# Key-weight transposes on TensorE, x tiles ahead on SyncE's queue, and a new order table in a two-attention kernel

## Chip, core and metric

One core of a Trainium2 chip. The metric is the device time of one launch in microseconds (us): the median of the runs of a kernel. The profiled execution is a run of its own, taken with the hardware profiler.

## What is computed

Two attention blocks on the same sequence of S = 2048 rows and D = 640 columns (32 heads of 20), mixed row by row by a gate. Cut to what matters:

```python
g = sigmoid((x * gate_w).sum(-1))            # one gate a row
# A: linear attention with a learned feature map
q, k, v = split(x @ wqkv)
pq, pk = q_h @ w_phi_h, k_h @ w_phi_h        # a 20x20 map for each head
phi = concat(softmax(p), softmax(-p))        # for pq and pk
a = (phi_q @ (phi_k^T v)) / (phi_q @ sum(phi_k)) @ A_wo
# B: 4 segments of 512 rows: causal softmax attention in the segment,
#    and a memory M, z of the segments before, read with elu(q)+1
b = (sigmoid(beta) * mem(q) + (1 - sigmoid(beta)) * softmax_attn(q, k, v)) @ B_wo
out = g * a + (1 - g) * b
```

## The kernel before

**Where things live.** x is held transposed in SBUF (`xT`, five blocks of 128 columns by 2048 rows). Tiles 0 to 3 (128 rows each) arrive as plain loads in `x_nat` and are transposed on TensorE against an identity matrix, five 128x128 blocks a tile into one PSUM bank (L681), then copied to `xT` on ScalarE or VectorE (L691, L693). Tiles 4 to 15 come by DMA transposes from DRAM (L569). Of PSUM's eight banks, four are one score tile (`st4`) and four (`w_76` to `w_79` in the profile) rotate among everything else.

**Block B.** `seg_in` projects a segment's four tiles on WkB, WqB and WvB (`proj`, L745: five matmuls of 320 columns for a half of the width); keys and queries are written to DRAM (`kd`, L764) and read back transposed (`kqT`, L1109). `b_qk` (L1138) makes scores into `st4`, one ScalarE exponential of 128x2048 turns them into `PT` (L1144), GpSimd masks the diagonal blocks (L1150), and `b_pv` (L1166) multiplies by the values.

**Block A.** The map w_phi is folded into the weights: for the keys, `WkA` = Wk x blockdiag(w_phi). A matmul wants the raw weights transposed as its stationary operand, so `wt_load` (L564) fetches them into `WT` by five DMA transposes of 128 columns each; `fold` (L730) makes ten groups of three matmuls against `WphiD`, the block-diagonal map that VectorE builds from `Wc` and a mask (L667), and ScalarE or VectorE evicts each group (L710, L712). The same happens for the queries later, through the same `WT`. `a1` projects the tiles on WvA and WkA, and `a3_num` and `fin` make the outputs.

**What sets the order.** Every operation is registered with an engine, a planned duration, what it reads and writes, and a number in the order of registration. `ORDER` is a table written out in the file: for each engine, the numbers in the order in which that engine shall run them ("73*3" is 73, 74, 75). The planner walks through these lists with its durations, gives each PSUM user the bank that is free first, and emits instructions in the order of the planned times. The engines run their own lists strictly in order and wait on semaphores. DMAs from SyncE (SP) and one from ScalarE use eight completion semaphores in turn, so that the ninth DMA waits for the first to land.

**The start.** ScalarE issues the first half of WkB. SP issues x tiles 0, 1, 2, then gate_w, half of WqB, Wc, beta, x tile 3, then the other halves of the weights. PE runs seven warm-up matmuls of 512 columns on a zeroed tile (L588) before tile 0 is transposed, and three more between the tiles.

Of the kernel before, what the change touches and what calls it, by code (L numbers as in the profile page):

```python
# [9 lines left out]
BF16 = mybir.dt.bfloat16  # L10
# [3 lines left out]
P = 128  # L14
# [13 lines left out]
        "29*7 73*3 77*2 80 88 104 89 82 120 90*2 105 121 92 106 94 122 95 107 123 96 108 124 126 "  # L28
        "97*2 127*2 136 129*2 137 110*2 142 112 138 113 143 114 144 139 192 145 193 140 146 176*2 "
        "194 178 195*2 84 208*2 179 210 224 170 225 180 226 171 227 211 228 212 164*2 172 166*2 "  # L30
        "173 152 174 158 153 168 154 159 155*2 160 182 161 230*2 183 261 232 162 184 262 185 263 "
        "186 233 264*2 234 362 426 363 427 364*3 428 368 400 369 429*2 464 401 465 402 198 370 "
        "403 199 371 200 372 404 201 466 509 214 202 247*2 215 467 216 249*2 254*2 468 256 251 "
        "257 512 258 458 217 240 218 241*2 459*4 243*2 394*2 276*3 292*3 396 284*3 397*2 308*3 "
        "288 280 312*2 289*2 314 296 281 297 282 298 661*3 838 664 839 665 840*2 749 842 750 655 "
        "751 656 300*2 657 304*2 302 306 516 752*2 374 658 375 381*2 659 376*2 383 378 384 406 "
        "385 527 814*2 649 816*2 650 818 413 651 414 407 415 408 416 409 417 520 410 521*2 652 "
        "530 523 671*2 438 673 439 674 445*3 440 448 675 441*2 543 449 693 703*3 694 706 695 707 "
        "696 709*4 775*2 697 777 477*2 778 479*2 779 481 546 470 713 471 534*3 472*2 537 474 850 "
        "857 851 858 852 859 853 860 854 550 861 687 828 688 829*2 737 689 738 690 677 739 691 "  # L40
        "740 678*2 741 680 831 681 832 743*2 561 882 745 883 746 889 884 747 885 890*2 886 892 "
        "876 893 877*2 564 879*2 432 921 433 914 434 915 922 435 923*2 436 916 925 719*4 577 490 "
        "917 554*3 491*2 723 493 557 918 494*2 499 496 500*3 580 902 953 903 954*2 904 908 905 "
        "909 934 956 910 906 957 911*2 584 935 568*4 946*2 1229 948 1230 949 1231 950 936*3 595 "
        "1232 1203 1233 940 791 941 1204*2 942 792 943 1206 944 1210 793 1207 1211*2 794 1213*2 "
        "598 1197 795 844 1198*2 845 725 846 1200 1342*3 847 1201 726 848 1345*2 611 727*3 588*3 "
        "870 591 807*3 975 810 976 871 977*2 614 811 602 872*2 603*2 874 605 731 643*4 618 732*4 "
        "966 759*2 967 761 968*2 1352 970 1353 971 762 972 763 629 1354*2 1261 1235*2 1262 1356 "
        "1242 1237 1263*2 1243 1238 1265 1244*2 781 1239 1246 632 622 782*2 623*2 1287*2 784 "
        "797*3 785 625 1289*2 800 1557*2 1291 1559 801 1560*2 995 1255*4 1267 1259 1268 1274 1269 "  # L50
        "1275 1270*2 1276*2 821 1278 822*2 998 1519*3 824*2 636*3 1522*2 639 1299*2 1446 1301*2 "
        "1430 1303 1447*2 1002 1431 1449*2 1432 1306*2 1433 1488*2 1308 1434 1490 1309 1491 1310 "
        "1492 1531 1017 765*4 1532 1538*2 1533 769 1540 1368*2 1534*2 1541*2 1020 1570*3 1370*3 "
        "1374*2 1006 1376*3 1007*4 1573*2 1563*5 1043 1384*3 1595 1387*2 1596 1223 1597 1602 "
        "1598*2 1224 1603*2 1225 1605 1226 1191 1606 1227 1192 1046 1193 1293 1194 1294 1336 1295 "
        "1025 1337 1026 1296*2 1027 1195 1338 1028 1339*2 1024 1319*7 1050 2409*5 1615 1462*2 "
        "1616*2 1464*2 1618 1634 1619 1466 1065 1328*4 1621 1635 1622 1589 1636*2 1623 1638 1590 "
        "1624 1591 1068 1592 1625 1055*2 1054 1057 1593 1058 1424*4 1091 1627*4 1390 1631 1428 "
        "1583 1391 1584*2 1392 1586 1179 1393 1587 1394 1094 1180*2 1358 1182 1359*2 1073 1361 "
        "1074*3 1362 1551 1072 1552*4 1098 2435*3 334*3 2438 330*3 322 2439 326 323 327 324 338 "  # L60
        "328 339*2 1113 346*3 350 342 351 343 1478 352 344 1479*3 1185*3 1482 1188 358*2 354*2 "
        "360 1116 356 1103*4 1102 1418*2 1412 1420*3 1413 1139 1525*3 1414 1528 2416*2 1529 2418 "
        "1415 1121 1416 2419 1122 2420 1123*2 1647*2 1120 1649 1656 1650 1657*2 1651*2 1659 1653 "
        "1142 1440*4 1472 1444 1473 1406 1474 1407*2 1502 1475*2 1503 1409*2 1495 1146 1504 1496 "
        "1505 1497 1506 1509*2 1498 2442 1499 1511*3 1456*2 1161 1458 2492 1459 2443 2493 1460 "
        "2444 2498 2445 2494 2446 2495*2 1670 1164 1400 2461*2 1401 2463 1666 2499 1402 2464 2500 "
        "2465 2501*2 1151 1403 1152 1672 1153 1668 2103 1154 1695*2 1404 1697*2 1169 1699 1170*2 "
        "1150 2106 1172 1681*3 1168 1684*2 1688*5 2110 2531*5 1709 1716 1710 1726*2 1717*3 1711 "
        "1728 1712 1729 2545 1713 2546*3 2125 1702*3 2549 1705 1759*4 2115*2 1706 2117*2 2114 "
        "2128 1888*3 1737 1891 1738 1892 1747*2 1739 2403 1749*2 2404 1740 2405*3 2151 2422*5 "  # L70
        "1769*4 2132*5 2154 2485*5 1780*2 1790 1782*2 1791*3 2479*5 2158 2467*5 1812 1802*2 1813 "
        "1804 1814*2 1805 2429*3 2505*2 2432*2 2173 2507*3 1895*3 1823*2 1898 1825*2 1899 1833*4 "
        "2511*3 2176 2514*2 2163*3 2162 2524 2166 2525*4 2455*4 2199 2459 1902*2 1866*4 1904*2 "
        "2180 1906 2181*4 2202 1845*4 1909*4 1855*2 1913 1857*2 1916*4 2206 1920 2552*4 2289 2556 "
        "2290 1876 2291 1877*3 2292*5 1923 2297*2 2221 1924*3 2301*3 1954*2 2304*4 1956*2 2308*3 "
        "2327*3 1944 2330*2 1945 1933*2 1946*2 2332 1935*2 2333*4 2224 2518*2 2448 2520 2449 2521 "
        "2450 2522 2451 2473*3 2452 2476*2 2247 2210 1987*3 2211 1990 2212*3 2229*4 2250 2391*4 "
        "2379*3 2228 2382*5 1976*2 2387*2 2254 1966 1978 1967*2 1979 1969 2341*3 2397*2 2344*5 "
        "2399 2349*2 2400 2269 2538*2 2315 2540 2316 2541 1997*2 2009 1999*2 2010 2317 2011 2318 "
        "2012 2542 2319*3 2272 2322*2 2019 2324 2020*3 2259*4 2258 2885 2787*9 2040*2 2796 2042*2 "  # L80
        "2030*4 2367*2 2888 2369*5 2062 2374 2063 2375 2064 2376 2065 2052*3 2277*2 2055 2279 "
        "2892 2594*2 2280 2596*2 2276 2598 2573*5 2775*3 2073*4 2907 2566*3 2083*2 2569*2 2085*2 "
        "2778*4 2897*2 2782 2899 2783 2900 2910 2784 2896 2580*3 2353*2 2583*2 2355*6 2601*2 2933 "
        "2603*2 2361*2 2611 2587 2612*3 2588*3 2915 2591 2916*3 2914 2936 3076*2 2801 3078 2802 "
        "3079 2803 2632 3080 2633*3 2622*2 2804 2624*2 2805*6 2940 3069 2644*4 2654 3070 2655*3 "
        "3071*3 2675*4 2955 2665*4 3083*3 2687*3 3086 2690 3087 2697*4 2958 2827*9 2708 2836 "
        "2709*3 2853*6 2718 2859*2 2719*3 2861*2 2981 2730 2740 2731 2741*3 2732 3090*3 2733 "
        "3093*2 2945*4 2984 2944 2963*4 2962 2865*4 2988 2869*5 2751*4 2813 2874 2814 3104 2815*3 "
        "3105 2818*3 3106*2 2821*2 3003 3097 2761*3 3114 2764 3098 3115 3099 3116*2 3100*2 2993*4 "
        "3006 2992 3278*3 3147 3281*2 3148 3283 3149 3284*3 3150 3287 3125*4 3029 2839*4 3135*2 "  # L90
        "2843 3137*2 2844*4 3157 2848 3158*3 3290*2 3032 3168*4 3292*4 3304*2 3296 3306 3297*3 "
        "3307*3 3178*4 3310 3200 3311 3201*3 3312*2 3190*4 3036 3011*4 3010 3211*4 3051 3221*4 "
        "3330*10 3233*3 3054 3243 3236 3244*3 3041*3 3316*3 3044 3319*5 3040 3324*2 3368*5 3254*4 "
        "3373 3264*4 3374*3 3059*2 3377 3061*2 3058 3342*6 3356*4 3348 3360 3349 3361 3350 3362*2 "
        "3351 3364*2 3381 3462 3435 3408 3383*6 3395 3389 3396 3422 3390 3397 3423 3391 3398*2 "
        "3410 3392 3400 3424*2 3401 3426 3411 3427 3412 3402*2 3428 3404 3429 3413 3430 3414 "
        "3449*2 3415 3431 3451 3437 3452 3416 3453 3438 3417 3454 3439 3455 3464 3418 3465 3456 "
        "3440 3466 3419 3457 3441 3467 3458 3442 3468*3 3443 3471 3444 3476 3472 3445 3477*2 3473 "
# [1290 lines left out]
```

The softmax here doesn't subtract the row's maximum and nothing guards it: scores larger than these inputs give would overflow.

## Time and profile before

| | |
|---|---|
| median of 3 runs | 291.14 us (291.12 to 291.29) |
| profiled execution | 290.81 us, of which the span of the trace is 289.1 |
| granted TensorE clock | 1.00 |
| TensorE (PE) busy | 281.2 us, 3777 matmuls |
| ScalarE (ACT) busy | 246.9 us |
| VectorE (DVE) busy | 229.6 us |
| GpSimd (POOL) busy | 189.0 us |
| SP's DMA queue | 37.39 MB, 58.5% of 16 DMA engines |

PE is the matmul engine and PEld its weight loads, which overlap it. "SPq" lines are DMA issues. A row of the timeline gives start, duration, engine, line, operation, tiles and shapes, and in brackets how long the engine had been idle before it and what ended that. A row of the windows gives a stretch, its length, the busy time of PE, PEld, DVE, ACT and POOL with the number of instructions, the granted clock, the DMA engines' share and GB/s. Matmuls are pipelined and their ends are modelled, so the spacing of their starts says more than their length. A tile's number in the profile is that of a buffer (`w_76` to `w_79` are the four banks, `st_75` is `st4`, `PT_119` a buffer of `PT`).

### The profile page before, as it was taken

The numbers are of one execution on the slowest core, as the hardware profiler recorded it, in microseconds if no ns is written. First come the engines' busy times: TensorE is split into PE (matmuls) and PEld (weight loads), VectorE is DVE, ScalarE is ACT, GpSimd is POOL, SyncE is SP. The second block draws the span as 40 slices with busy tenths as digits, with TensorE's granted clock in tenths as the row PEclk, the third lists the DMA queues.
The fourth block names the chain that finished last, engine by engine and source line by source line (L and its number), as shares of the span: only waits on it lengthen the run. The fifth ranks groups of instructions, "written<-read, shape, count | busy, mean of one in ns | idle before, by whom it ended". The sixth has DMA issues, their size and how long they took to land.

```text
span 289.1 us, 9813 instructions
## 1 busy us (share of the span) xinstructions
PE 281.2 (97%) x3777; PEld 191.9 (66%) x3777; DVE 229.6 (79%) x850; ACT 246.9 (85%) x353; POOL 189.0 (65%) x333
## 2 busy tenths in 40 slices
PE   7999999999999999999999999999999999999995
PEld 3676676576676667677766566567766657667873
DVE  0774477887789989689968999998998999999720
ACT  3356799998999999999899999998999999988222
POOL 7045379789965899778282858474866586688600
DMA  7997795845815442615059684834874749564342
GB/s 219 314 220 153 108 253 73 153 101 103 122 39 142 124 114 75 93 64 123 4 128 267 121 195 119 161 82 131 171 153 115 137 106 207 118 113 118 105 107 63
DMA packets 87976, 38.42 MB, mean 133 GB/s; under 512 B 69882, under 2 KB 83834, under 8 KB 87930
## 3 DMA queue, kind: packets, MB, share of 16 engines
q1 hardware_dynamic: 87274, 37.39, 58.5%
q8 instruction: 29, 0.48, 0.7%
q10 hardware_dynamic: 656, 0.41, 0.5%
q14 instruction: 17, 0.14, 0.2%
HBM read 5.61 MB, written 15.60 MB: 73 GB/s over the span
## 4 chain that ended last, share of the span: by engine, by line
PE 84%; DVE 11%; DMA 2%; issue 1%; POOL 1%; ACT 0%; DVEq 0%
PE w_78 L745 10%; PE w_79 L745 10%; PE w_76 L745 9%; PE w_77 L745 9%; PE st_75 L1138 8%; PE w_79 L1086 5%; PE w_77 L1166 3%; PE w_78 L1086 3%; PE w_76 L1086 3%; PE w_77 L1086 3%; PE w_76 L1166 3%; PE w_78 L1166 2%; DVE ts_3003 L1044 2%; PE w_78 L988 2%; PE w_76 L988 2%; PE w_77 L988 2%
## 5 line engine op out<-in xcount | busy, mean ns | idle before, releaser
L745 PEld LDWEIGHTS <-xT 128*128 128x128 bf16 x800 | 72.4, 97 | 34.0 <-issue 9.1
L1144 ACT ACTIVATE PT_119<-st_75 128x2048 bf16<-128x2048 f32 x14 | 26.4, 1889 | 1.3 <-PE st_75 L1138 1.1
L1144 ACT ACTIVATE PT_120<-st_75 128x2048 bf16<-128x2048 f32 x14 | 26.6, 1898 | 0.1
L1144 ACT ACTIVATE PT_123<-st_75 128x2048 bf16<-128x2048 f32 x13 | 24.6, 1892 | 1.7 <-PE st_75 L1138 1.4
L1144 ACT ACTIVATE PT_121<-st_75 128x2048 bf16<-128x2048 f32 x13 | 24.6, 1890 | 0.9 <-PE st_75 L1138 0.9
L1144 ACT ACTIVATE PT_124<-st_75 128x2048 bf16<-128x2048 f32 x13 | 24.5, 1888 | 0.7 <-PE st_75 L1138 0.3
L1144 ACT ACTIVATE PT_122<-st_75 128x2048 bf16<-128x2048 f32 x13 | 24.7, 1897 | 0.3
L1150 POOL TENSOR_SCALAR_AFFINE_SELECT PT_121<-PT_121 128x512 bf16<-128x512 bf16 x21 | 13.3, 638 | 12.7 <-DVE phik_103 L775 6.1
L1150 POOL TENSOR_SCALAR_AFFINE_SELECT PT_124<-PT_124 128x512 bf16<-128x512 bf16 x21 | 13.3, 637 | 11.7 <-DVE phiq_114 L1120 5.1
L1150 POOL TENSOR_SCALAR_AFFINE_SELECT PT_119<-PT_119 128x512 bf16<-128x512 bf16 x22 | 13.8, 637 | 6.4 <-ACT PT_119 L1144 4.6
L1150 POOL TENSOR_SCALAR_AFFINE_SELECT PT_120<-PT_120 128x512 bf16<-128x512 bf16 x23 | 14.6, 639 | 4.3 <-ACT kq_94 L710 1.4
L1166 PEld LDWEIGHTS <-PT_119 128*128 128x128 bf16 x224 | 15.6, 96 | 0.8 <-issue 0.2
L1166 PEld LDWEIGHTS <-PT_120 128*128 128x128 bf16 x224 | 15.5, 96 | 0.7 <-POOL PT_122 L1150 0.2
L1150 POOL TENSOR_SCALAR_AFFINE_SELECT PT_123<-PT_123 128x512 bf16<-128x512 bf16 x21 | 13.2, 637 | 4.1 <-DVE phiq_116 L1120 2.3
L1166 PEld LDWEIGHTS <-PT_124 128*128 128x128 bf16 x208 | 14.6, 96 | 1.1 <-issue 0.2
L1166 PEld LDWEIGHTS <-PT_122 128*128 128x128 bf16 x208 | 14.2, 96 | 1.1 <-POOL PT_124 L1150 0.2
L1166 PEld LDWEIGHTS <-PT_121 128*128 128x128 bf16 x208 | 14.4, 96 | 0.7 <-issue 0.2
L1166 PEld LDWEIGHTS <-PT_123 128*128 128x128 bf16 x208 | 14.1, 96 | 0.9
L745 PE MATMUL w_78<-WqB,xT 128*128 128x320 bf16 x60 | 14.5, 299 | 0.1
L1150 POOL TENSOR_SCALAR_AFFINE_SELECT PT_122<-PT_122 128x512 bf16<-128x512 bf16 x20 | 12.5, 637 | 2.2 <-DVE phiq_114 L1120 1.0
L859 DVE TENSOR_REDUCE ksum_163<-Ek_155 128x32 f32<-128x640 bf16 x16 | 12.6, 801 | 1.7 <-ACT Ek_155 L852 1.6
L745 PE MATMUL w_77<-WvB,xT 128*128 128x321 bf16 (+1 forms) x55 | 13.2, 300 | 0.0
(685 smaller groups left out, 1138.6 us busy)
## 6 DMA issues: line engine op xcount, KB each, us to landing
out_dram<-osb_3016 SPq DMA_DIRECT2D x12, 80.0 KB, 2.2
WqB<-in_B_wq_dram SPq DMA_DIRECT2D x2, 400.0 KB, 4.7
WvB<-in_B_wv_dram SPq DMA_DIRECT2D x2, 400.0 KB, 4.2
WvA<-in_A_wqkv_dram SPq DMA_DIRECT2D x1, 800.0 KB, 6.4
WoA<-in_A_wo_dram SPq DMA_DIRECT2D x1, 800.0 KB, 5.1
WoB<-in_B_wo_dram SPq DMA_DIRECT2D x1, 800.0 KB, 6.5
out_dram<-osb_3018 SPq DMA_DIRECT2D x10, 80.0 KB, 1.8
out_dram<-osb_3017 SPq DMA_DIRECT2D x10, 80.0 KB, 1.8
```

What stands on the lines that cost most here:

```text
L745: nc.tensor.matmul(w[:, 0:width], lhsT=T["xT"][:, c, sc * P:(sc + 1) * P], rhs=T[Wn][:, c, lo:lo + width], start=(c == 0), stop=(c == KC - 1))
L859: op("DVE", 0.74, lambda sgn=sgn: nc.vector.tensor_reduce(out=T["ksum"][js][:, H * sgn:H * sgn + H], in_=T["Ek"][ik][:, sgn].rearrange("p ...
L988: nc.tensor.matmul(w, lhsT=T["WqA"][:, c, t * P:(t + 1) * P], rhs=T["xT"][:, c, s * L:(s + 1) * L], start=(c == 0), stop=(c == KC - 1))
L1044: op("DVE", dve_t(320), lambda w, c3=c3, qt=qt: nc.vector.tensor_tensor(out=T["ts"][d][:, :, 8 * (qt % 2):8 * (qt % 2) + 8], in0=vw(w)[:, ...
L1086: nc.tensor.matmul(w[:, 0:320], lhsT=T[nm][j][:, k5, :], rhs=T[Wo][:, k5, hf * 320:hf * 320 + 320], start=(i == 0), stop=(i == 9))
L1138: nc.tensor.matmul(st4[:, i, o:o + w], lhsT=T["kqT"][j][r:r + 32, 0, c * P:(c + 1) * P], rhs=T["kqT"][j][r:r + 32, 1, c * P:L], start=True ...
L1144: op("ACT", act_t(2048), lambda: nc.scalar.activation(out=T["PT"][slot], in_=st4, func=ACT.Exp, scale=SCALE_B), r=("st4",), w=(("PT", slot ...
L1150: nc.gpsimd.affine_select(out=v, in_=v, pattern=[[0, 4], [1, P]], compare_op=ALU.is_ge, fill=0.0, base=0, channel_multiplier=-1)
L1166: nc.tensor.matmul(w[:, j * 84 + i * V1:j * 84 + (i + 1) * V1], lhsT=T["PT"][slot][:, i, o + (j - c) * P:o + (j - c + 1) * P], rhs=T["vB"] ...
```

## The change

The raw key weights are fetched by one plain load into `WqA` (the buffer that the folded query weights will fill later), and TensorE transposes them there, 25 blocks of 128x128 in five groups (`fold_tr`), each group copied from its bank to `WT` on ScalarE or VectorE. The raw query weights still come by DMA, as one DMA transpose of 640x640 in place of five. `WT` is one object for the waits now, no longer five slices. The planned durations of the transposes of x and of the three later warm-up matmuls are halved; this changes no instruction by itself. The order table is new: since one DMA is registered earlier, most numbers are one higher. In the new list SP issues Wc, x tiles 0 to 3, half of WqB, beta, the second halves of WkB and WqB, half of WvB, gate_w and the other half of WvB.

```diff
     "PE":
-        "29*7 73*3 77*2 80 88 104 89 82 120 90*2 105 121 92 106 94 122 95 107 123 96 108 124 126 "
+        "30*7 74*3 78*2 81 83 89*2 105 91*2 106 93 107 111 108 137 112*2 121 109 138 114 122 139 "
...
     "SP":
-        "1*3 10 5 11 13 4 8 7 6 9 100 132 116 148 12 272 507 273 271 274*2 14 508 220 15*3 541 "
+        "11 1*5 14 6*3 10 9 117 133 101 149 12*2 508*2 15 542 16 221 189 17 205 18 237 543 668 "
...
+    dma(wload("WqA", A_wqkv[:, D:2 * D]), (), ("WqA",), -9, 819, release=18.0)
...
-    def wt_load(base, key, rel):
-        for t in range(KC):
-            dma(lambda t=t: nc.sync.dma_start_transpose(
-                out=T["WT"][:, t, :], in_=A_wqkv[:, base + t * P:base + (t + 1) * P]),
-                (), (("WT", t),), key + 0.1 * t, 164, tr=True, release=rel)
+    def wt_load(nm, base, key, rel):
+        dma(lambda: nc.sync.dma_start_transpose(out=T["WT"], in_=A_wqkv[:, base:base + D]),
+            (), ("WT",), key, 819, tr=True, release=rel, issue=4.2)
...
-    def warm(n):
+    def warm(n, t=0.43):
...
-        op("PE", 0.5, f, r=("xn%d" % sc, "ident_b"), w=("st4",), alloc=bk, key=-1000 + sc)
-        warm((2, 1, 0, 0)[sc])
+        op("PE", 0.28 if sc else 0.42, f, r=("xn%d" % sc, "ident_b"), w=("st4",), alloc=bk, key=-1000 + sc)
+        warm((2, 1, 0, 0)[sc], 0.22)
...
+    def fold_tr(key):
+        for t in range(KC):
+            bk = bank()
+
+            def f(w, t=t):
+                for ic in range(KC):
+                    nc.tensor.transpose(out=w.bitcast(BF16)[:, ic * P:(ic + 1) * P],
+                                        in_=T["WqA"][:, ic, t * P:(t + 1) * P],
+                                        identity=T["ident_b"])
+            op("PE", 5 * 0.064, f, r=("WqA", "ident_b"), alloc=bk, key=key)
+            op(AD, (0.59, 0.4), copy_to(lambda w, t=t: (T["WT"][:, t, :],
+                                                        w.bitcast(BF16)[:, 0:D])),
+               acc=("WT",), free=bk, key=key)
...
-                    op("PE", pe_t(m * DH), f, r=(("WT", t), ("WphiD", t)), key=key, **kw)
+                    op("PE", pe_t(m * DH), f, r=("WT", ("WphiD", t)), key=key, **kw)
...
-    wt_load(D, -1899, 11.5)
+    fold_tr(-11)
     fold("k", "WkA", -10)
-    op("X", 0.0, None, w=("WqA",))
-    wt_load(0, -1800, 60.0)
+    wt_load("q", 0, -1800, 60.0)
```

## The prediction

> **What bounds the kernel now.** I read the busy shares first, then the slices, then the chain that ended last.
>
> ```profile
> PE 281.2 (97%) x3777; PEld 191.9 (66%) x3777; DVE 229.6 (79%) x850; ACT 246.9 (85%) x353; POOL 189.0 (65%) x333
> PE   7999999999999999999999999999999999999995
> DMA  7997795845815442615059684834874749564342
> PE 84%; DVE 11%; DMA 2%; issue 1%; POOL 1%; ACT 0%; DVEq 0%
> ```
>
> TensorE is busy in every slice but the first and the last, and 84% of the chain is its own. A busy PE need not be PE at its peak, so I looked at starts: in the timeline from 8 to 20 us the 320-column matmuls start 0.135 us apart, one upon another. There is no slack under which PE work could hide: a matmul more costs its spacing, and only idle PE can be won back. The windows (span, PE, PEld, DVE, ACT, POOL busy) say where that is:
>
> ```profile
> 0.00:10.00 10.00, 7.53 (x48) 4.06 (x49) 2.65 (x8) 3.38 (x6) 5.25 (x27) 1.00 0.88 250
> 10.00:20.00 10.00, 10.00 (x76) 7.04 (x74) 7.53 (x24) 5.30 (x15) 2.76 (x12) 1.00 1.04 266
> 20.00:30.00 10.00, 10.00 (x84) 6.53 (x82) 5.27 (x19) 7.00 (x12) 6.24 (x30) 1.00 0.68 143
> 30.00:40.00 10.00, 9.61 (x102) 6.71 (x100) 5.59 (x16) 8.26 (x16) 3.74 (x12) 1.00 0.93 192
> 160.00:180.00 20.00, 19.33 (x275) 12.41 (x273) 18.64 (x91) 19.83 (x24) 14.71 (x23) 1.00 0.63 135
> 220.00:240.00 20.00, 19.41 (x251) 12.54 (x249) 18.34 (x90) 20.00 (x25) 13.26 (x21) 1.00 0.58 118
> ```
>
> The prologue has 2.47 us idle, 1.26 of them before PE's first instruction. From 10 to 280 us all windows together have 2.4 us. The chain in order of time and the timeline show the prologue's hole:
>
> ```profile
> 0.81 3.74 DMA WkB<-in_B_wk_dram
> 4.57 3.19 DMA x_nat<-in_A_x_dram
> 7.80 0.45 PE w_77 L681 x5
> ```
>
> ```profile
> 5.56 0.44 PE L681 MATMUL w_78<-ident_b,x_nat 128*128 128x128 bf16 x5
> 5.84 0.30 PE L745 MATMUL w_79<-WkB,xT 128*128 128x320 bf16 x1
> 7.79 0.28 PEld L681 LDWEIGHTS <-x_nat 128*128 128x128 bf16 x5 [1.39 <-DMA x_nat<-in_A_x_dram]
> ```
>
> The fourth x tile is the ninth DMA, and with eight completion semaphores in rotation its issue waits for the first, WkB's half, to land (4.57). It lands near 7.75. Until PE runs unbroken (8.03) it has done all transposes but only three of the 20 matmuls WkB x xT.
>
> **What the Trainium skill says.** *TensorE: Matmul & The Clock Gate*, "Wait — 56ns, not 53.3ns?": 128 columns start 55.6 ns apart at the full clock, 106.7 cold. The trace agrees: the five above take 0.44 us, of which the last is 0.22, so (0.44 - 0.22)/4 = 55 ns; the first pair at 4.23 us is 106 ns apart. *DMA: Bandwidth & Descriptors*, "Issuing engines are not separate DMA queues": DMAs of SP and ACT run on the same 16 engines and interleave. The packet records here agree on the sharing but not on the interleaving: tile 0 moves first (1.83 to 2.7), then ACT's half of WkB (2.5 to 4.1), and tiles 1 and 2, issued at 1.27 and 1.73, only from 3.75, as if in one line in order of issue. The same page, "Queues, rings and completion order": a completion is written only after every earlier write of that DMA engine. WvA's last row moves at 19.0 but the landing shows at 20.82, with transposing DMAs behind it, so a plain load beside such DMAs may be told late.
>
> **The change, part by part.**
>
> *25 transposes more on PE* (`fold_tr`): 25 x 0.0555 = **+1.4 us**, at a place (20 to 30 us) where PE is at 10.00 of 10. Nothing covers it. Bounds: 1.2 (a few fall into idle PE) and 2.2 (0.44/5 each, if groups of five do not overlap).
>
> *Five evictions more of 640 columns*: two on ACT at 0.69 (the xT copy) and three on DVE at 0.48, 1.4 us on each. Cover: from 20 to 40 us ACT is busy 15.3 and DVE 10.9 of 20. Taken 0. They use the same four PSUM banks as the projections, and each fold matmul now reads all of WT, not its own slice: the first fold matmul stands 18 matmuls (2.4 us) behind the last transpose, while DVE's list has about 2.9 us between its first and last WT copy. 0 to +0.6, taken within the fold below.
>
> *Prologue.* SP's listing in the changed kernel begins with Wc, then the four x tiles, WqB's half, beta. So x is not strictly first: Wc's 640 packets of 40 B (0.55 us, 5.91 to 6.46, in the trace) stand ahead, and x tile 0, issued at about 1.34 and no more at 0.82, now comes behind ACT's 400 KB of WkB. By the line above, each tile takes 0.44 us of all engines (1 and 2 took 0.95) and is usable 0.45 after its last packet: WkB to 4.1, tile 0 to 4.55, usable **5.0** (PE took it at 4.23), tile 3 to 5.9, usable **6.35** (was 7.8). Then: tile 0's transposes end 5.5, ACT's copy 0.69 ends 6.2, and 0.25 later the first projection: 6.45. Tiles 1 to 3 follow on DVE at 0.48 each with one WphiD (0.30) between, ready near 7.0, 7.5, 8.3. PE was unbroken from 8.03 with three matmuls done, that is as if from 7.63; now from 6.45: 1.2 us. Off go 0.3 (the fourth group needs tile 3 at 7.9, and the third bank's eviction queues behind that copy on DVE) and 0.2 for late weights: WqB's half lands near 7.5 and is needed by the ninth matmul at 7.55; WvB's second half lands near 12.2, needed near 11.9; gw_row comes within 0.1 of its use. **-0.7 us.** Bounds: 0 (Wc or the weights later) and -1.5 (tile 0 still ahead of WkB, so used at 4.23; then WqB holds the gain). Warm-up matmuls are as many as before; the planned clock changes no instruction.
>
> *DMA transposes of the key weights go.*
>
> ```profile
> 14.90 1.28 SPq L564 DMA_TRANSPOSE WT<-in_A_wqkv_dram  x1
> 16.36 2.20 SPq L1109 DMA_TRANSPOSE kqT_110<-kd_60  x1
> 18.61 6.21 SPq L564 DMA_TRANSPOSE WT<-in_A_wqkv_dram  x4
> 24.86 1.28 SPq L569 DMA_TRANSPOSE xT<-in_A_x_dram  x1
> ```
>
> SP gets back 1.28 + 6.21 = 7.5 us of issue and pays 0.43 for one plain load of WqA. What stood behind, xT tile 4 and kqT_111, starts some 6 us sooner, but PE waits for neither before or after: 0. WqA is issued after WvA and moves behind it, done near 21.5; told late as WvA was, 23; the first transpose needs it near 23. 0 to +0.5, taken **+0.2**. The query weights' five issues (57.6 to about 78, 1.2 to 2.1 us each) become one of perhaps 6 in one piece; behind it wait kqT loads with over 10 us in hand, and its reader is near 128 us. 0, at most +0.3.
>
> *Fold.* PE stutters on its banks:
>
> ```profile
> 31.99 0.20 PE L730 MATMUL w_76<-WphiD,WT 128*128 128x80 bf16 x1 [0.21 <-DVE WkA L712]
> ```
>
> Between 29.9 and 32.2 the starts lie 1.0 us further apart than their columns need. The new list mixes one to three fold matmuls with projections, which gives each bank time, but adds the WT wait above. **-0.2**, between -0.9 and +0.6.
>
> *New order table.* The listings of both, multiplied by the spacing of each width, put the 80 score groups (`b_qk`) at nearly the same PE work: from the 28th to the 59th, 1.1 to 2.1 us later, mostly 1.4, which is the transposes. So the late stages keep their form, and their DVE-bound waits (0.67 and 0.59 us above). 0, bounds -1.2 and +1.2.
>
> Sum: +1.4 - 0.7 + 0.2 - 0.2 = **+0.7 us**. The profiled execution took 290.81 (span 289.1 and 1.7 around it), so 291.5 by its own time; the median of the runs, 291.14, lies 0.33 above it: **291.8**.
>
> **The rivals.** *Faster*: the list takes the stutter out of the fold (1.0, not 0.2) and half of the late waits (1.2): +0.7 - 0.8 - 1.2 = -1.3, 289.8. For it: the fold's matmuls are spread; against: the late lists hardly move, and DVE does the same work there. It decides once more than 1.3 us beyond my sum are saved. *Cancelled*: tile 0 is not held by WkB, or the fold wait goes alone, and the transposes are just paid: 0, 291.1. *Worse*: the prologue wins nothing, as x now waits for WkB and Wc, and WqA and WT come late (0.5 + 0.6): +2.5, 293.6. That the change does not do what it says holds in one point, x not being first, and is in my sum.
>
> **How the numbers follow.** A measurement of this kernel can tell about 0.2%, 0.6 us, from no change. My forecast with its own spread (+0.6 to +1.6) has 0.33, worse 0.15, cancelled 0.28, faster 0.24. The range 290.0 to 293.5 leaves out the far ends of faster and worse. Slower by over 0.2%: 0.33 + 0.15 = 0.48; within 0.28; faster 0.24.
>
> **What would show it.** x_nat's first transpose near 5.0 and its last group near 6.4 to 6.8; PE unbroken from about 6.5, with short waits near 8 and 12; fold_tr's five groups at 0.44 each near 23 to 26; matmul count 3802; the score groups from the 28th on later by 0.5 to 1. Wrong if tile 0 is used at 4.2, if PE idles over 1 us between 10 and 30 us, or if the windows after 100 us lose or win more than 1 us.

## The result, and the profile after

The changed kernel takes 292.77 us (median of 4 runs, 291.94 to 293.05), the kernel before 291.16 us in the same job (291.12 to 291.29). The ratio is 1.005 (95% interval 1.0029 to 1.0071): about 1.6 us slower, where +0.7 was forecast. The profiled execution took 292.64 us with a span of 290.9, against 290.81 and 289.1. The last matmul starts at 287.52 us, before at 285.77: 1.76 us later.

On the page, TensorE's busy time is about the same and the chain that ended last (followed back from the last instruction) has changed: PE's own share fell from 84% to 71%.

```profile
PE 280.9 (97%) x3789; PEld 192.7 (66%) x3802; DVE 229.0 (79%) x853; ACT 247.7 (85%) x355; POOL 190.3 (65%) x333
PE 71%; DVE 18%; DMA 5%; issue 3%; SPq 1%; ACT 1%; DVEq 0%; ACTq 0%
```

(The forecast's 3802 matmuls are there by PEld's weight loads; 13 matmul records are missing.) The same windows as before (span, then PE, PEld, DVE, ACT, POOL busy) say where:

```profile
0.00:10.00 10.00, 8.02 (x54) 4.60 (x55) 2.85 (x7) 2.31 (x4) 5.14 (x26) 1.00 0.85 244
10.00:20.00 10.00, 8.71 (x63) 5.88 (x62) 6.08 (x24) 4.22 (x12) 2.07 (x11) 1.00 0.79 251
20.00:30.00 10.00, 9.23 (x84) 6.56 (x83) 2.94 (x10) 5.86 (x14) 5.59 (x27) 1.00 1.01 202
30.00:40.00 10.00, 10.00 (x105) 6.95 (x104) 7.78 (x24) 9.52 (x19) 3.57 (x11) 1.00 0.86 166
160.00:180.00 20.00, 19.45 (x261) 12.11 (x257) 18.20 (x91) 20.00 (x25) 14.86 (x23) 1.00 0.70 157
220.00:240.00 20.00, 19.57 (x244) 11.85 (x246) 18.30 (x89) 19.96 (x28) 12.60 (x18) 1.00 0.62 123
```

From 10 to 20 us PE is busy 8.71 where it was 10.00, and from 20 to 30 us 9.23 where it was 10.00. From 30 to 40 us it is at 10.00, where it was 9.61, and the late windows are as they were. The timeline has the holes (line numbers are those of each run's own kernel):

```profile
5.05 0.45 PE L678 MATMUL w_76<-ident_b,x_nat 128*128 128x128 bf16 x5 [0.72 <-DMA x_nat<-in_A_x_dram]
...
6.57 2.10 SPq L552 DMA_DIRECT2D gw_row<-in_gate_w_dram  x1
8.71 0.39 SPq L527 DMA_DIRECT2D WvB<-in_B_wv_dram  x1
...
12.61 0.17 PE L696 MATMUL w_79<-ident_b,gw_row 5*128 5x5 bf16 x1 [1.01 <-DMA gw_row<-in_gate_w_dram]
13.62 0.18 DVE L699 COPY WvB<-w_79 128x5 bf16<-128x5 bf16 x1 [2.69 <-DMA WvB<-in_B_wv_dram]
13.85 0.30 PE L756 MATMUL w_79<-WkB,xT 128*128 128x320 bf16 x1 [0.28 <-DVE WvB L699]
...
15.52 0.33 SPq L775 DMA_DIRECT2D kd_60<-kq_96  x1
15.90 0.43 SPq L527 DMA_DIRECT2D WvA<-in_A_wqkv_dram  x1
...
22.48 0.30 PE L756 MATMUL w_77<-WvA,xT 128*128 128x300 bf16 x1 [0.77 <-DMA WvA<-in_A_wqkv_dram]
```

Tile 0 is used at 5.05, as forecast. Then PE waits three times: for gate_w (whose issue kept SP for 2.10 us and the second load of WvB behind it until 8.71), for bank `w_79`, and for WvA, which in both kernels SP issues behind the fourth store of the first segment's keys and queries. That store is issued at 15.52 where it was at 14.04: the first store comes earlier than before (10.37 against 11.23), and the first two waits, 1.61 us together, lie between the first and the fourth. So the wait for WvA follows in part from the other two. Its landing is also told late: its packets end near 20.3, and the landing shows at 22.43. The middle wait is indirect: the bank holds the transposed gate column, DVE's copy of that column (L699) writes into the tile `WvB` and so waits for WvB's loads, and the next projection on WkB waits for the copy.

To size the waits I took, for every matmul, the distance to the next start less what its columns need (0.135 us for 320), and summed it:

| stretch, us | before | after |
|---|---|---|
| 0 to 10 | 3.14 | 2.28 |
| 10 to 20 | 0.20 | 1.78 |
| 20 to 30 | 0.75 | 1.20 |
| 30 to 40 | 1.29 | 0.64 |
| sum | 5.38 | 5.90 |

The three waits are 1.17, 0.44 and 0.94 us long by this measure. With the transposes at 1.34 (measured below) the first 40 us cost 5.90 - 5.38 + 1.34 = +1.86, and the last matmul starts 1.76 later: after 40 us next to nothing is lost or won in sum. In between the new order moves things about: from the third score group on, the groups start 0.67 to 2.67 us later than before.

### The profile page after: what moved, and what is told of

It reads as the page before. It is cut to its first block, busy times and chain, and to the rows that moved or that the text cites. A ratio compares the mean times of both kernels' runs of the same rounds, so it can differ in the third digit from the quotient of the medians.

```text
span 290.9 us, 9842 instructions
## 1 busy us (share of the span) xinstructions
PE 280.9 (97%) x3789; PEld 192.7 (66%) x3802; DVE 229.0 (79%) x853; ACT 247.7 (85%) x355; POOL 190.3 (65%) x333
## 4 chain that ended last, share of the span: by engine, by line
PE 71%; DVE 18%; DMA 5%; issue 3%; SPq 1%; ACT 1%; DVEq 0%; ACTq 0%
PE w_76 L756 9%; PE w_78 L756 8%; PE w_79 L756 8%; PE w_77 L756 8%; PE st_75 L1149 7%; PE w_79 L1097 3%; PE w_78 L1097 3%; PE w_77 L1177 3%; PE w_77 L1097 3%; PE w_76 L1097 2%; DMA WvA<-in_A_wqkv_dram 2%; DVE ts_3028 L1055 2%; DVE ts_3029 L1055 2%; PE w_79 L1177 2%; PE w_78 L1177 2%
## 5 line engine op out<-in xcount | busy, mean ns | idle before, releaser
L1161 POOL TENSOR_SCALAR_AFFINE_SELECT PT_122<-PT_122 128x512 bf16<-128x512 bf16 x20 | 12.6, 635 | 8.5 <-DVE xx_3020 L1043 3.5
L756 PE MATMUL w_79<-WkB,xT 128*128 128x320 bf16 x50 | 13.3, 298 | 0.6 <-DVE ts_3028 L1055 0.3
L999 PE MATMUL w_77<-xT,WqA 128*128 128x512 bf16 x42 | 13.2, 379 | 0.4
L870 DVE TENSOR_REDUCE ksum_163<-Ek_155 128x32 f32<-128x640 bf16 x16 | 12.6, 805 | 0.5 <-ACT Ek_155 L863 0.5
```

What stands on the lines that cost most here:

```text
L756: nc.tensor.matmul(w[:, 0:width], lhsT=T["xT"][:, c, sc * P:(sc + 1) * P], rhs=T[Wn][:, c, lo:lo + width], start=(c == 0), stop=(c == KC - 1))
L870: op("DVE", 0.74, lambda sgn=sgn: nc.vector.tensor_reduce(out=T["ksum"][js][:, H * sgn:H * sgn + H], in_=T["Ek"][ik][:, sgn].rearrange("p ...
L999: nc.tensor.matmul(w, lhsT=T["WqA"][:, c, t * P:(t + 1) * P], rhs=T["xT"][:, c, s * L:(s + 1) * L], start=(c == 0), stop=(c == KC - 1))
L1161: nc.gpsimd.affine_select(out=v, in_=v, pattern=[[0, 4], [1, P]], compare_op=ALU.is_ge, fill=0.0, base=0, channel_multiplier=-1)
```

## The experiments

Theory at the outset: the transposes are paid in full and the new weight waits eat the prologue's gain. Rival: the new order table loses the time later. Where a short diff shows a list of numbers, only SP's list changes. In the changed kernel's numbering 1 to 4 are the x tiles, 5 and 7 WqB's halves, 6 WkB's second half, 8 and 9 WvB's halves, 10 gate_w, 11 Wc, 12 WvA, 13 the raw key weights, 14 beta, and 117, 133, 101, 149 the first segment's stores (in the kernel before, 4 is x tile 3, 8 and 9 WvB's halves, 10 gate_w, 11 Wc, 13 beta). Each ratio is to the kernel before, timed in the same job; its medians went from 291.04 to 291.47 over the jobs. The changed kernel was timed in the first job alone, so a difference between medians of two jobs is uncertain by some 0.4 us, and I lean on the traces (one execution of each) and on the ratios.

**e1: gate_w early.**

```diff
-        "11 1*5 14 6*3 10 9 117 133 101 149 12*2
+        "11 1*4 10 5 14 6*3 9 117 133 101 149 12*2
```

> The changed kernel with one entry moved in SP's list: gate_w (gw_row) right behind the four x tiles. The other engines' lists stay. Theory A (the loss is waits for small and late loads in the prologue): PE's wait of 1.17 us before the gw_row transpose and most of the 0.44 us for WvB's second half go, 1.3 to 1.6 us in the span, so about 291.3. Rival B (the transposes and the new late order cost it, and early waits are taken back later): within 0.4 us of the changed kernel, about 292.5.

292.82 us, ratio 1.0071 (1.0056 to 1.0086): nothing gained. The gate_w wait went, and the bank wait in its place grew to 1.6 us, because the copy L699 now started at 13.97, later than 13.62. With gate_w out of the way, it was the second load of WvB that took long to issue, at the same time:

```profile
6.83 1.96 SPq L527 DMA_DIRECT2D WvB<-in_B_wv_dram  x1
```

So the long issue is not gate_w's own. WvA's projections started at 22.45, and every one of the 80 score groups and the last matmul stand within 0.02 us of the changed kernel's.

**e2: Wc behind x.**

```diff
-        "11 1*5 14 6*3 10 9 117
+        "1*5 11 14 6*3 10 9 117
```

> The changed kernel with Wc moved in SP's list from ahead of the x tiles to behind half of WqB, so that x is strictly first. If Wc ahead puts tile 0 behind ScalarE's half of WkB: tile 0 is used at 4.2 and no more at 5.05, the projections start 0.5 to 0.8 us sooner. But gw_row still comes where it came, so theory A expects its wait to grow by as much and the time to stay within 0.3 us of 292.8. Rival: the 0.8 us are kept, 292.0.

291.87 us, ratio 1.0025 (1.0014 to 1.0036): 0.9 us better than the changed kernel by the medians (0.8 when each is taken against the kernel before of its own job), 0.51 in the trace, all of it by 22 us. Neither gate_w nor WvB took long to issue (0.47 and 0.45). Tile 0 is used at 4.22 without a wait, L699 runs at 12.83, and WvA's projections start at 21.97. A wait of 0.54 us is new at 7.6: DVE builds `WphiD` from Wc ahead of tile 3's copy.

**e3: both.**

```diff
-        "11 1*5 14 6*3 10 9 117
+        "1*4 10 5 11 14 6*3 9 117
```

> Both moves in SP's list: x tiles 0 to 3, gw_row, half of WqB, Wc, beta and the rest. Theory A: the saving of the first move, and now up to 0.8 us of the second beside it, unless the wait for half of WqB takes it: 290.5 to 291.3. Rival B: 292.0 to 292.5.

292.59 us, ratio 1.0046 (1.0033 to 1.0060). The two do not add: the second load of WvB took 1.82 us to issue at 6.88, its last packet ended at 13.26 (12.19 in e2), L699 ran at 13.87 and WvA's projections at 22.51, all groups again within 0.04 us of the changed kernel.

**e4: every key-weight transpose twice.**

```diff
-                for ic in range(KC):
+                for ic in 2 * tuple(range(KC)):
```

> The changed kernel with each of the 25 key-weight transposes issued twice into the same place; nothing else moves. The price of 25 transposes by itself: 25 x 55 ns = 1.4 us if nothing covers them, 294.2; 2.2 us (0.44 for each five) if groups do not overlap with what follows, 295.0; 0 to 0.5 if they fall into time in which PE waits, 293.0.

293.97 us, ratio 1.0101 (1.0086 to 1.0116): +1.2 on the medians. In its profiled execution the end is 2.60 later, but 1.26 of that is there when WvA's projections start (23.74 against 22.48: PE's matmuls kept their slow first spacing, 0.267 us for 320 columns, until 10.4). The other **1.34** us are 25 transposes at 54 ns.

These four changed the theory. In them, whatever was moved before 22 us, the rest of the kernel followed as one piece: shifts at the end of -0.02, -0.51, +0.03 and +2.60 where WvA's projections (transposes apart) shifted by -0.03, -0.51, +0.03 and +1.26. What is late last before that point sets the end.

**e5: the kernel before with x tile 3 fourth on SP's queue**, the x part of the change alone.

```diff
-        "1*3 10 5 11 13 4 8 7 6 9 100
+        "1*4 10 5 11 13 8 7 6 9 100
```

> The kernel before with x tile 3 put fourth on SP's queue and nothing else moved: x strictly first, no transposes on TensorE, old order of the engines. If what bounds the prologue of before was tile 3's late issue, the 1.39 us wait ahead of its transposes goes; but PE's own list has only three projections before these transposes, so at most about 1 us can be won: 290.1 to 290.6. Theory that earlier waits only trade places until the first projections of block A (WvA's landing behind the kd stores): no gain beyond 0.3 us, 290.9 to 291.3, with PE waiting somewhere between 8 and 22 us for a weight that is now a place later.

291.42 us against 291.37, ratio 1.0005 (0.9997 to 1.0013): nothing, as the second theory had it, but not for its reason alone. The 1.22 us hole of before is cut to 0.62, and still the first score group comes 0.30 later. One part of this is that PE stayed at the slow spacing longer. In the kernel before, it is fast from 4.4 us, and tile 1's five transposes take 0.44; here it is slow until 5.92:

```profile
5.60 0.68 PE L681 MATMUL w<-ident_b,x_nat 128*128 128x128 bf16 x5
```

After 4 us the slow spacing costs 0.91 us here and 0.11 before, so more than the hole gave back, and PE is ready for WvA at 20.98 where it was ready at 20.80. The other part is WvA itself, which lands at 21.12 and no more at 20.82:

```profile
21.16 0.88 PEld L745 LDWEIGHTS <-xT 128*128 128x128 bf16 x8 [0.36 <-DMA WvA<-in_A_wqkv_dram]
```

In the kernel before, WvA lands 0.02 us after PE is ready for it, so an earlier PE had nothing to win there as long as WvA landed at that time. That WvA took e5's gain is not shown, since PE did not come early.

**e7: WvA ahead of the last two stores**, in the changed kernel.

```diff
-        "... 10 9 117 133 101 149 12*2
+        "... 10 9 117 133 12 101 149 13
```

> The changed kernel with the load of WvA moved on SP's queue ahead of the last two stores of the first segment's keys and queries, nothing else moved. Theory (WvA's landing sets when everything after 22 us starts, and the rest is rigid): the 0.94 us wait goes, all score groups and the last matmul move 0.7 to 0.95 us earlier alike, 291.8 to 292.1. Rival (the wait is covered again by another, e.g. the raw key weights or a late reload behind the two stores): 292.5 to 293.0, with a new wait of about the same length between 22 and 60 us.

292.57 us, ratio 1.0035 (1.0021 to 1.0049). In the trace the wait for WvA is gone, and all groups and the last matmul come 0.78 to 0.80 earlier, in the forecast's range. The medians gave 0.2 only (0.4 with each taken against the kernel before of its own job), with runs from 291.78 to 292.82, so by the times alone this gain is not shown.

**e8: the waits in one go.**

```diff
-        "11 1*5 14 6*3 10 9 117 133 101 149 12*2
+        "1*4 11 5 14 6 7 10 9 8 117 133 12 101 149 13
```

> The changed kernel with x really first (Wc behind the four tiles), gate_w and the half of WvB that is read first each a place earlier, and WvA ahead of the last two stores. Theory: with WvA no longer binding, the prologue's waits (tile 0's 0.72, gate_w's 1.17, WvB's 0.44) count one for one; the WphiD wait on Wc (0.5) comes in their place; net 1.3 to 2.3 us below the changed kernel, 290.4 to 291.4. Rival (a later thing binds whatever is done before): no more than the kernel with WvA alone, 291.8 to 292.1.

291.03 us against 291.37 for before, ratio 0.9987 (0.9979 to 0.9996), the last matmul and every score group 1.83 to 1.84 earlier than in the changed kernel. Its timeline:

```profile
12.60 0.43 SPq L527 DMA_DIRECT2D WvA<-in_A_wqkv_dram  x1
12.74 0.18 DVE L699 COPY WvB<-w 128x5 bf16<-128x5 bf16 x1 [1.57 <-DMA WvB<-in_B_wv_dram]
...
20.66 0.56 PE L756 MATMUL w<-WvA,xT 128*128 128x300 bf16 x3
```

WvA's projections stand at 20.66 with no wait, and what is left is L699. With SP's queue in this order the kernel is 0.3 us under before although it pays for the transposes; the next two runs price these.

**e10: e8 with every transpose twice.**

```diff
-                for ic in range(KC):
+                for ic in 2 * tuple(range(KC)):
```

> The kernel with x first and the weights earlier on SP's queue (e8), with each of the 25 transposes of the raw key weights issued twice and nothing else changed. Theory (PE has no slack there, and the rest of the kernel is rigid): 25 times 54 ns, the end 1.3 to 1.4 us later than in e8, in the trace alike from the second score group to the last matmul; 292.3 to 292.5 by the median. Rival (part of the transposes falls into idle PE or is won back later): less than 1.0 us.

292.41 us, ratio 1.0038 (1.0025 to 1.0051), 1.38 above e8. In the trace the end is 1.62 later, 0.28 of it by WvA's projections (20.94), so 1.34 again. A group of ten takes 0.72 where five take 0.44: (0.72 - 0.44)/5 = 56 ns.

```profile
24.05 0.72 PE L724 MATMUL w<-ident_b,WqA 128*128 128x128 bf16 x10
```

**e11: e8 with the key weights transposed by DMA.** The 25 transposes and five evictions are left out, and the DMA writes WT itself.

```diff
-    dma(wload("WqA", A_wqkv[:, D:2 * D]), (), ("WqA",), ...
+    dma(lambda: nc.sync.dma_start_transpose(out=T["WT"], in_=A_wqkv[:, D:2 * D]), (), ("WqA",), ...
-            op("PE", 5 * 0.064, f, ...
-            op(AD, (0.59, 0.4), copy_to(...), ...
+            op("PE", 0.0, None, ...
+            op(AD, 0.0, None, ...
```

> The kernel e8 with the transposes of the raw key weights given back to the DMA engines: one DMA transpose of 640x640 into WT takes the place of the plain load into WqA, and the 25 PE transposes and their five evictions are left out; all orders stay. If the DMA's issue (about 6 us at 15) still ends before the stores of keys and queries have landed, the 1.35 us of the transposes come back whole: 289.5 to 289.9, below both kernels. Rival (the change to TensorE was needed: the DMA transpose delays the reload of keys and queries behind it on SP's queue, or comes late for the fold): PE waits at the first score group near 26 us or at the first fold near 30 us, and the gain is below 0.7 us or turned into a loss, 290.4 to 292.

289.70 us, ratio 0.9960 (0.9938 to 0.9982), 1.33 below e8 by the medians and 1.39 at the last matmul. Three of its seven runs took 290.87 to 291.67, the others 289.43 to 289.70; why is open. SP's queue:

```profile
15.18 5.65 SPq L557 DMA_TRANSPOSE WT<-in_A_wqkv_dram  x1
21.01 2.59 SPq L1120 DMA_TRANSPOSE kqT<-kd  x2
```

The issue fills time in which SP would have waited for the stores to land (in e8 the reload of keys and queries starts at 19.47), and moves that reload by 1.5 us. The first score group starts at 25.52 without a wait for it, and the first fold matmul finds WT there. So nothing was seen to wait for the DMA transpose. The rest did not follow as one piece this time: WvA's projections start 0.16 later than in e8, PE has new holes of 0.22 us at 26.7 and 0.28 at 34.5, the score groups from the fourth to the 55th come only 0.77 to 0.83 earlier, and the remainder is won later, 0.35 of it behind the last group. The net gain near 1.3 is measured; that it equals the 1.34 of the transposes is in part chance.

**e12: e8 with beta behind WvB.**

```diff
-        "1*4 11 5 14 6 7 10 9 8 117
+        "1*4 11 5 6 7 10 9 8 14 117
```

> The kernel e8 with the load of beta moved behind the halves of WvB on SP's queue. If the 0.39 us wait for WvB's second half at 13 us is one of the order of issue, it shrinks as WvB is issued some 0.5 us earlier: 290.6 to 291.0, the late score groups 0.2 to 0.4 us earlier than in e8. Rival (WvB comes when the DMA engines have moved the bytes, not when it is issued): the wait stays, 290.9 to 291.2.

290.74 us, ratio 0.9976 (0.9967 to 0.9985), 0.3 below e8 by the medians, as the first theory had it; but the trace shows 0.04 at the end. L699 ran at 12.51 against 12.74, and PE, which came 0.45 earlier, waited 0.61 and 0.17 us. The slow spacing after 4 us cost PE 0.48 us here and 0.96 in e8, which is about the 0.45; that beta's place made PE earlier is not shown. The two theories are not parted by it.

**e13: e11 and e12 together.** 

> The two edits that won time over e8 together: the raw key weights transposed by one DMA (as in e11) and beta behind WvB (as in e12). If they add, 0.3 us below e11: 289.4, between 289.2 and 289.7. Rival (WvB's landing near 12.7 us caps both): as e11, 289.7.

289.61 us, ratio 0.9940 (0.9925 to 0.9955): 0.1 below e11 by the medians (0.29 at the last matmul in the traces), so a further gain is not shown by the times. It is the fastest here, 1.6 us under before and about 3.2 under the changed kernel.

**e14: e12 with WvB in one load.**

```diff
-    wpart("WvB", B_wv, 0, -1994, "WvBw", eng="SP")
-    wpart("WvB", B_wv, 1, -1993, "WvBw", eng="SP")
+    dma(None, (), (("WvBw", 0),), -1994, 305)
+    dma(wload("WvB", B_wv), (), (("WvBw", 1),), -1993, 610)
```

> e12 with WvB fetched by one load of 800 KB in place of its two halves, so that 400 KB more stand before the half that TensorE reads first; one issue fewer. From 1.8 to 12.6 us the DMA engines move 309 to 316 GB/s in every kernel so far, with a busy share above 1. Theory (the first 13 us are bound by the bytes that the DMA engines can move): 410 KB at 315 GB/s, the wait at 12 us longer by 1.3 us and the end later by about as much less what the single issue saves, 291.6 to 292.2. Rival (bound by issue on SP or by the latency of a load): no later than e12, 290.5 to 290.9.

290.50 us, ratio 0.9973 (0.9963 to 0.9983): no later, and my theory of it fell. The copy waits for both halves however they are cut:

```profile
12.38 0.18 DVE L699 COPY WvB<-w 128x5 bf16<-128x5 bf16 x1 [1.58 <-DMA WvB<-in_B_wv_dram]
```

In the kernels with two loads the last of their packets ends at 11.84 to 13.32, and L699 starts about 0.6 to 0.67 us after it where it waits for WvB (changed kernel 13.02 and 13.62, e1 13.32 and 13.97, e8 12.11 and 12.74, e12 11.86 and 12.51). So the order of the halves, which I had turned round for e8, could not matter, and this run says nothing on whether bytes bind. The windows from 1.8 to 12.6 us do, as far as a busy share goes (last two columns: DMA share, GB/s). Before, after and e12, one each:

```profile
1.80:12.60 10.80, 9.59 (x67) 5.67 (x66) 4.44 (x14) 4.20 (x9) 4.60 (x23) 1.00 1.05 309
```

```profile
1.80:12.60 10.80, 9.09 (x64) 5.26 (x62) 3.22 (x8) 3.74 (x9) 4.02 (x19) 1.00 1.05 310
```

```profile
1.80:12.60 10.80, 10.49 (x70) 6.29 (x69) 3.31 (x10) 3.60 (x9) 4.04 (x19) 1.00 1.07 316
```

In all three the DMA engines have work for the whole stretch at nearly one rate. But the expectation's "309 to 316 GB/s in every kernel so far" is wrong: in e1, e3, e4, e5 and e7 the stretch shows 286 to 299 GB/s, and there the last WvB packet ends at 12.95 to 13.32; in e2, e8, e11, e12 and e13 it shows 315 to 318, and the packet ends at 11.84 to 12.23. Nearly the same bytes move in all of these up to that packet, so a low rate and a late packet are much the same fact, and neither explains the other. Four x tiles and six halves of weights are 4 x 164 + 6 x 410 = 3.1 MB; at 316 GB/s from 1.83 that is 11.7 us, where e12's last WvB packet ends at 11.86. That an early start of PE runs into this supply was not tested by taking bytes away; it stays a reading. Why WvB's last packet is at 13.0 in the changed kernel is open in part: between 6 and 8 us its DMA engines moved 277 GB/s (e1 236, e12 348), in the stretch in which SP's issue of gate_w took 2.10 us (1.96 for WvB in e1). (348 - 277) x 2 us is 142 KB, 0.45 us of the 1.2. Which of the two causes the other was not tried.

## Why the prediction was right or wrong

The sign and the case (slower) were right and 292.77 is within the range; the size, +0.7, was less than half of the +1.6 that came, and one of its own signs of being wrong came true: PE idles 1.29 + 0.77 us between 10 and 30 us, over 1 us. By its steps:

- **25 transposes, +1.4: right.** 1.34 in two pairs of traces, 1.2 and 1.38 by medians. PE has no slack there. The price in *TensorE: Matmul & The Clock Gate*, "Wait — 56ns, not 53.3ns?" (55.6 ns) agrees with the 54 ns measured.
- **Evictions and fold, -0.2: the sign right, too small.** From 30 to 40 us the loss fell from 1.29 to 0.64, and 20 to 30 us without the WvA wait from 0.75 to 0.26, about 1.1 us together. The stretches do not hold the same matmuls in both kernels and no run changes the fold alone, so this is an estimate. The wait on all of `WT` did not appear: PE is at 10.00 in that window.
- **Prologue, -0.7: the step that failed.** Tile 0 was right to 0.05 us. PE is unbroken from 6.82, against 6.45 forecast: 0.81 won and not 1.2. The failing term is "Off go ... 0.2 for late weights". It cost 1.17 + 0.44 = 1.61 us. I had gate_w "within 0.1 of its use", not seeing its issue stretch to 2.10 us with WvB behind it, and I priced WvB for its own projections, not for the copy that writes a column of the same tile and holds a bank until both loads are in. From 0 to 20 us the loss is 4.06 against 3.34: +0.7 and not -0.7.
- **WqA late, +0.2: wrong weight.** The raw key weights were not waited for. WvA was, by 0.94 us: I moved WqA past WvA in the sum and never priced that WvA itself stands behind the fourth store, which the waits of the prologue make late: WvA is issued at 15.90 and no longer at 14.42.
- **Order table 0, query weights 0, SP's freed issue time 0: right.** The late stages changed by about 0.1 us in sum. No run has the new order without the transposes or the other way round, so that the order costs nothing late is read from the traces alone. (The fifth of the query weights' issues before is at 89.69, not by 78; nothing hangs on it.)

So +1.34 + 0.72 + 0.94 - 1.14 = +1.86 by 40 us, and 1.76 at the end. The errors on the prologue and WvA (1.4 + 0.7) were partly hidden by the fold's (0.9). Without that the sum would have stood at +2.8 or 293.9, outside the range, so that the range held is in part luck. The *faster* rival had the fold right and the late waits wrong; *worse* named the late weights but the wrong ones; that x was not strictly first held, and putting it first (e2) won 0.5 in the trace and 0.8 to 0.9 by the medians.

## What to carry to other kernels

When a prologue is fed by loads that keep the DMA engines full, an early start of the compute engine is worth only what the last load before the steady state allows: list for each weight when its bytes end and when it is needed, and move the one that binds last (here WvA, behind stores that nobody waited for so soon). Look also at small writes into a tile that is being loaded: a copy of one column waited for all of the tile's loads and kept a bank from the next matmul. And work given to an engine without slack is paid whole (1.34 us here); a DMA transpose issued into an idle stretch of SP's queue was waited for by nobody.

## What had not been expected of the hardware

- The issue of a load on SP that starts at 6.6 to 6.9 us took 2.10 us for gate_w's 1.3 KB in the changed kernel, 1.96, 1.82 and 1.85 for WvB's 400 KB in e1, e3 and e5, and 0.47 for gate_w at 6.80 in e2, all while 400 KB loads were moving. It is not tied to the load; what sets it is open.
- One DMA transpose of 640x640 took SP 5.65 us to issue in e11 (3.6 to 6.4 over the runs); five of 128 columns took 7.5 us together before.
- From a load's last packet to the start of the DVE copy that waits for it passed about 0.6 to 0.67 us in every kernel where it waited.
- WvA's landing is told 1.7 to 2.3 us after its last packet in the kernels that issue it behind all four stores, and 0.3 to 0.9 in those that issue it two stores earlier (e7 to e14). Why is open.
- Matmuls start at half pace at first (0.267 us apart for 320 columns, 107 ns for 128), and in these executions for how long differs: such a start is last seen at 3.4 us in the changed kernel, e1 and e7, at 3.8 in e14, at 4.3 before, at 4.6 to 4.8 in e2 and e11 to e13, at 5.9 to 6.0 in e5, e8 and e10, at 7.1 in e3 and at 10.3 in e4, while the granted clock reads 1.00 in all. PE waited for tile 0 alike in e4 (0.93 us) and e1 and e7 (0.94 and 0.89). With one trace of each kernel, whether it goes with the kernel or with the execution is open.
